# Expert weight loads of an up-projection spread out: at most two a step from step 25 to 30 in place of five at once

## The chip, the cores and the metric

One Trainium2 chip; the kernel runs on one of its cores. The metric is device time in microseconds (us). A core has five engines that run their own instruction streams and meet on semaphores: PE (TensorE, matmuls and transposes into PSUM), DVE (VectorE), ACT (ScalarE), POOL (GpSimd) and SP (SyncE), which here issues every DMA. "PEld" is the load of the stationary operand of a matmul.

## The reference, cut to what matters

Causal attention with a decay, a SiLU feed-forward layer, and a soft mixture of eight experts with four slots each, in fp32. `x` is 2304 tokens by 512.

```python
# attention (4 x 8 heads, 576 tokens, head 64) -> x (2304, 512)
h = x @ w_in                      # (2304, 2048)
g = h * (1.0 / (1.0 + np.exp(-h)))
x = g @ w_out                     # (2304, 512)

logits = x @ phi                  # 32 slots
d = softmax(logits, over tokens); c = softmax(logits, over slots)
slot_input = d.T @ x
for e in range(8):
    h = np.maximum(slot_input[e] @ w1[e], 0.0)     # w1[e]: 512 x 1024
    slot_out[e] = h @ w2[e]                        # w2[e]: 1024 x 512
return c @ slot_out
```

## The kernel before, in words

Attention comes first. The feed-forward layer is then run as 36 steps: nine chunks of 256 tokens times four groups of 512 hidden columns; a step is a pair (c, fg) and has a number k. Chunks 0 to 3 are interleaved in steps 0 to 15, and from step 16 on chunk 4 + (k - 16) // 4 is worked on, so that steps 24 to 27 are chunk 6, 28 to 31 chunk 7 and 32 to 35 chunk 8. The second matrix product is not carried out per token: `w_out` and `phi` are multiplied beforehand (tiles WP), and each step's `g` is used twice, for the logits (`lp`) and for the slot sums (`pp`).

A step on PE is: 24 matmuls `h` (two halves of 12, L593 to L595: three partial products of split operands), then `stacked(k)`: matmuls `lp` (L664) of the pieces that were made ready by the step before, perhaps `pp` (L780) for a whole chunk, and then `square(k)`: transposes `gtp` and small softmax pieces. ACT and DVE turn `h` into `gt` (L607, L614).

`lp` needs `g` transposed. There are two ways to it. `g_tr` transposes on PE (`gtp`, L637) and ACT copies the result into a tile `gr` (L638). The far way goes without PE: DVE transposes blocks of 32 by 32 into `gb` (`blocks`, L646), a DMA writes `gb` to a buffer `far` in HBM (L649), and four DMAs of 128 KB each bring it back as `gr` with the blocks in place (`placed`, L655). In steps 17 to 27 one or two pieces a step go the far way. `turn_far(k)`, at the end of `square(k)`, transposes them and issues the writes; `place(k + 1)`, in `stacked(k + 1)`, issues the reads; and `lp` of `stacked(k + 2)` uses them. Up to step 24 `gb` has a page of its own; from step 25 on it comes from a ring of two buffers (pool `w0`, tag `t`), which it shares with the `gr` of `g_tr`.

The pages: an allocator by hand, a list FREE of 4 KB-a-partition pages, first in, first out; `page()` takes one, `release()` gives it back when the last use has been recorded. `gt`, far `gr`, `xh`/`xl` (the split input) and the `unit` tiles all come from it.

A unit is 512 KB of weights for the tail: first eight that hold `w_out` (WO, written to HBM earlier), then 32 of `w1` and 32 of `w2`. `load_unit` (L442 for WO, L448 for `w1`, L450 for `w2`) issues one DMA on SP. How many may have been issued is set by the table ROOM, pairs of a step and a count, which is looked up at the end of each step:

```python
mo["umax"] = max([0] + [n for at, n in ROOM if k + 1 >= at])
pump()        # while len(WR) + len(units) < umax and FREE: load_unit()
```

All DMAs are on SP's queue in the order in which the program records them: reads, writes and units behind each other. Eight counters (DMAHW0 to DMAHW7) are given to them in turn, and an issue waits until the DMA that had the same counter eight issues before has landed. After step 35 the tail computes the experts (`h` L851 from `w1`, `so` L913 from `w2`) and combines.

Of the kernel before, what the change touches and what calls it, by code (L numbers as in the profile page):

```python
# [27 lines left out]
RATE = 1.5  # L28
CAPS = ((0, 12), (5, 6))
LAG = 1  # L30
ROOM = ((18, 5), (20, 6), (21, 7), (22, 10), (24, 11), (25, 12), (26, 17), (28, 19), (30, 23), (32, 29), (33, 32), (34, 35), (35, 42), (36, 45))
PARTS = ((0, 256, {}), (256, 128, {0: 1, 3: 2, 5: 2, 7: 2}), (384, 128, {1: 3, 3: 2, 5: 2, 7: 1}))
RING_A, RING_B, RING_T = "014", "235", "b"

# [2 lines left out]
def tile_attention_moe_softmoe(ctx: ExitStack, tc: tile.TileContext, qk, vr, f, wcat, phi, w1, w2, out):  # L37
# [394 lines left out]
    def pump():  # L432
        while mo["next"] < mo["last"] and mo["raws"] < mo["cap"] and len(FREE) > mo["spare"]:
            conv_dma()
        while len(WR) + len(units) < mo["umax"] and FREE:
            load_unit()
# [362 lines left out]
    def ct_page(c):  # L799
        t = page([96, 1024], "ct", F32R)[0]  # L800
        CTP.append(t)
        CT.update((c + k, t[:, 256 * k:256 * k + 256]) for k in range(4))
# [182 lines left out]
    with tc.manual_schedule():  # L985
# [156 lines left out]
        for k, (c, fg) in enumerate(steps):  # L1142
# [46 lines left out]
            if last:  # L1189
                ct_page(0)  # L1190
                ct_page(4)
            mo["umax"] = max([0] + [n for at, n in ROOM if k + 1 >= at])
            pump()
# [59 lines left out]
```

## Time and profile before

| | us |
|---|---|
| median of 3 runs | 536.84 |
| lowest and highest | 536.3, 539.62 |
| the profiled execution | 534.77 |
| its span, first to last instruction | 533.1 |
| PE busy in the span | 507.7 |
| mean granted TensorE clock, share of full | 0.994 |

The rows further down are from the profiled execution, 2.07 us below the median of the runs. Times in them count from the start of its span. Matmuls are pipelined and their ends are modelled, so each starts before the row before it has ended. A row with x8 is eight instructions merged, and its length includes the waits between them. In brackets stands how long the engine was idle before the row and what ended that.

### The profile page before, as it was taken

How to read it: one execution, taken by the hardware profiler on the slowest of the kernel's cores; microseconds unless marked ns; L12 is line 12 of the kernel's file. 1: busy time of each engine (PE TensorE's matmuls, PEld its weight loads, DVE VectorE, ACT ScalarE, POOL GpSimd, SP SyncE). 2: the span in 40 equal slices, each digit the busy share in tenths (PEclk: the TensorE clock that was granted, in tenths of full speed). 3: DMA queues.
4: the chain of work that ended last, by engine and by line, in shares of the span. 5: the costliest groups of instructions: out<-in, count | busy, mean ns of one | idle time of the engine just before them, and what ended most of it. 6: DMA issues, size and time to landing. Idle time of an engine off the chain costs nothing.

```text
span 533.1 us, 11562 instructions
## 1 busy us (share of the span) xinstructions
PE 507.7 (95%) x4285; PEld 373.7 (70%) x4285; DVE 336.6 (63%) x895; ACT 295.4 (55%) x586; POOL 208.4 (39%) x228
## 2 busy tenths in 40 slices
PE   8899999999999999899999999999998999999995
PEld 4687877787777787587777777757575667665563
DVE  6766777677789299999989534655654431434023
ACT  8798889889886675556645544323321333341012
POOL 9777788888788314447565300000000000001000
PEclk9999999999999999999999999999998999999998
DMA  5727656665553397213431119699697719767998
GB/s 145 222 79 204 194 169 172 180 190 156 147 173 96 110 347 287 80 41 101 137 119 79 41 49 317 188 297 260 229 333 204 256 65 337 254 255 302 408 405 310
DMA packets 44109, 105.83 MB, mean 199 GB/s; under 512 B 8180, under 2 KB 17172, under 8 KB 44052
## 3 DMA queue, kind: packets, MB, share of 16 engines
q1 hardware_dynamic: 44052, 105.08, 60.4%
q8 instruction: 34, 0.56, 0.4%
q14 instruction: 23, 0.19, 0.1%
HBM read 82.58 MB, written 17.52 MB: 188 GB/s over the span
## 4 chain that ended last, share of the span: by engine, by line
PE 61%; DMA 13%; DVE 11%; ACT 6%; POOL 3%; issue 3%; SPq 2%; DVEq 0%; POOLq 0%; ACTq 0%
PE h L593 8%; PE h L595 8%; PE h L594 8%; PE av L304 5%; DMA gr<-far 4%; PE st L247 3%; PE gtp L637 3%; PE mx L201 3%; PE lp L664 3%; PE rs L288 3%; PE st L249 3%; PE h L851 3%; PE pp L780 3%; PE so L913 3%; DMA QA<-mr 2%
## 5 line engine op out<-in xcount | busy, mean ns | idle before, releaser
L593 PE MATMUL h<-w,xh 128*128 128x512 f32 x288 | 118.8, 413 | 3.3 <-DVE gt L614 3.3
L595 PE MATMUL h<-w,xh 128*128 128x512 f32 x288 | 113.7, 395 | 0.0
L594 PE MATMUL h<-w,xl 128*128 128x512 f32 x288 | 113.5, 394 | 0.0
L614 DVE SCALAR_TENSOR_TENSOR gt<-gt,h 128x512 f32<-128x512 f32 (+1 forms) x73 | 48.4, 675 | 66.4 <-ACT gt L607 66.4
L607 ACT ACTIVATE gt<-h 128x512 f32<-128x512 f32 (+1 forms) x73 | 42.7, 589 | 80.6 <-PE h L595 68.8
L826 POOL MEMSET SM<- 128x512 f32 x2 | 1.1, 529 | 177.1 <-ACT gt L607 174.5
L253 ACT ACTIVATE E<-st 128x256 f32<-128x256 f32 (+4 forms) x160 | 63.2, 430 | 12.4 <-PE st L249 10.6
L593 PEld LDWEIGHTS h<-w,xh 128*128 128x128 f32 x288 | 54.2, 188 | 21.3 <-DVE gt L614 7.2
L207 DVE CUSTOM_DVE_ANT_0 junk<-mx,mask 128x64 bf16<-128x64 f32 (+3 forms) x128 | 49.9, 415 | 30.4 <-PE mx L201 27.5
L595 PEld LDWEIGHTS h<-w,xh 128*128 128x128 f32 x288 | 54.2, 188 | 12.7
L594 PEld LDWEIGHTS h<-w,xl 128*128 128x128 f32 x288 | 54.3, 189 | 10.8
L247 PE MATMUL st<-QA,KA 128*128 128x256 f32 (+2 forms) x192 | 55.7, 301 | 5.8 <-ACT E L253 2.8
L249 PE MATMUL st<-QB,KB 128*128 128x256 f32 (+2 forms) x192 | 51.6, 294 | 0.0
L201 PE MATMUL mx<-KA,QA 127*128 127x64 f32 (+2 forms) x192 | 49.7, 325 | 1.5 <-DVE Mt L207 0.7
L270 POOL TENSOR_SCALAR_AFFINE_SELECT E<-E 128x256 f32<-128x256 f32 (+1 forms) x96 | 40.9, 440 | 25.9 <-ACT E L253 24.5
L304 PE MATMUL av<-E,VF 128*64 128x320 f32 (+4 forms) x448 | 50.8, 364 | 0.0
L179 POOL TENSOR_TENSOR QB<-qk,QA 64x576 fp32r<-64x576 f32 x30 | 42.8, 1429 | 2.3
L177 POOL TENSOR_TENSOR KB<-qk,KB 64x576 fp32r<-64x576 f32 x30 | 42.2, 1425 | 1.7 <-ACT KB L171 0.6
L304 PEld LDWEIGHTS av<-E,VF 128*64 128x64 f32 x448 | 29.6, 137 | 17.8 <-POOL E L270 0.3
L247 PEld LDWEIGHTS st<-QA,KA 128*128 128x128 f32 x192 | 34.6, 180 | 10.5 <-ACT E L253 8.0
L524 POOL TENSOR_TENSOR raw<-raw 128x512 f32<-128x512 f32 x16 | 26.8, 1675 | 37.1 <-ACT raw L513 30.0
L201 PEld LDWEIGHTS mx<-KA,QA 127*128 127x128 f32 x192 | 32.8, 189 | 5.5 <-DVE Mt L207 2.0
(155 smaller groups left out, 854.5 us busy)
## 6 DMA issues: line engine op xcount, KB each, us to landing
unit<-in_w_dram SPq DMA_DIRECT2D x64, 512.0 KB
raw<-in_w_dram SPq DMA_DIRECT2D x32, 512.0 KB
far<-gb SPq DMA_DIRECT2D x16, 512.0 KB
gr<-far SPq DMA_DIRECT2D x64, 128.0 KB
qk<-in_qk_dram SPq DMA_DIRECT2D x14, 576.0 KB
VF<-in_v_dram SPq DMA_DIRECT2D x16, 320.0 KB
RB<-R SPq DMA_DIRECT2D x32, 144.0 KB
WO<-wt SPq DMA_DIRECT2D x8, 512.0 KB
```

What stands on the lines that cost most here:

```text
L179: eng.tensor_tensor(QB.of(p)[64:128, h], src[0:64], QA[p % 3][0:64, h, 64:640], ALU.subtract)
L201: nc.tensor.matmul(t[:, 0:w], lhsT=qa[0:127, h, 128 * blk:128 * blk + 128], rhs=ka[0:127, h, k0:k0 + w], start=True, stop=True)
L207: nc.vector.tensor_tensor_reduce(out=junk[:, 0:w], in0=t[:, 0:w], in1=mask[:, 448 - w:448], scale=1.0, scalar=Mx[p][:, h] if j == 5 else - ...
L247: nc.tensor.matmul(t[0:m, o:o + n], lhsT=ka[:, h, k0:k0 + m], rhs=qa[:, h, 64 + q0:64 + q1], start=True, stop=False)
L249: nc.tensor.matmul(t[0:m, o:o + n], lhsT=kb_[:, h, k0:k0 + m], rhs=qb[:, h, q0:q1], start=False, stop=True)
L253: nc.scalar.activation(e[0:m], t[0:m, 0:o], AF.Exp, scale=0.125)
L304: nc.tensor.matmul(AVP[p][x][64 * h:64 * h + 64, o0:o0 + n], lhsT=VF[p % 2][:, kb, h], rhs=E[2 * p + h][kb][:, c:c + n], start=kb == 0, st ...
L593: nc.tensor.matmul(o, lhsT=xh[:, d, tok], rhs=w[:, 0], start=(d == 0), stop=False)
L594: nc.tensor.matmul(o, lhsT=xl[:, d, tok], rhs=w[:, 0], start=False, stop=False)
L595: nc.tensor.matmul(o, lhsT=xh[:, d, tok], rhs=w[:, 1], start=False, stop=(d == 3))
L607: nc.scalar.activation(GT[c, fg][:, t, n * j:n * j + n], G[c, fg, t][:, n * j:n * j + n], AF.Tanh, scale=0.5)
L614: nc.vector.scalar_tensor_tensor(g, g, 1.0, h[:, n * j:n * j + n], op0=ALU.add, op1=ALU.mult)
```

## The change

The table ROOM is written anew between steps 26 and 31; nothing else differs. At the end of step 25 the count is 14 in place of 17, then 16 (17), 18 (19), 19 (19), 21 (23) and 23 (23) at the ends of steps 26 to 30. From step 31 on both tables are equal.

```diff
-ROOM = ((18, 5), (20, 6), (21, 7), (22, 10), (24, 11), (25, 12), (26, 17), (28, 19), (30, 23), (32, 29), (33, 32), (34, 35), (35, 42), (36, 45))
+ROOM = ((18, 5), (20, 6), (21, 7), (22, 10), (24, 11), (25, 12), (26, 14), (27, 16), (28, 18), (29, 19), (30, 21), (31, 23), (32, 29), (33, 32), (34, 35), (35, 42), (36, 45))
```

What SP's queue holds from the end of step 25 to step 28, before. `far<-gb` are the writes of the far way, `gr<-far` the reads (four a piece), `unit` the weight loads. The first row is the write of step 25, the five loads end that step, the four reads and two writes belong to step 26, the next three rows to step 27, and the last to step 28:

```order
L649 DMA far<-gb 128x1024
L448 DMA unit<-in_w_dram 128x1024 x5
L655 DMA gr<-far 32x4x256 x4
L649 DMA far<-gb 128x1024 x2
L655 DMA gr<-far 32x4x256 x8
L649 DMA far<-gb 128x1024
L448 DMA unit<-in_w_dram 128x1024 x2
L655 DMA gr<-far 32x4x256 x4
```

The same place on SP's queue in the changed program, from the write of step 25 on:

```order
L649 DMA far<-gb 128x1024
L448 DMA unit<-in_w_dram 128x1024 x2
L655 DMA gr<-far 32x4x256 x4
L649 DMA far<-gb 128x1024 x2
L448 DMA unit<-in_w_dram 128x1024 x2
L655 DMA gr<-far 32x4x256 x8
L649 DMA far<-gb 128x1024
L448 DMA unit<-in_w_dram 128x1024 x2
L655 DMA gr<-far 32x4x256 x4
```

Three loads have left the place ahead of the four reads of step 26, and two stand now between the two writes of step 26 and the eight reads of step 27, where there was none.

DVE executes the same instructions in the same order. What they wait for differs at the two transpositions of step 26 (a piece of the difference, the program before with -, the changed one with +; in brackets the counters waited for: DMAHW are landings, PE, DVE and Activation count instructions of these engines):

```order
 L797 TENSOR_TENSOR arena<-arena 128x64 [waits DVE_49]
 L646 STREAM_TRANSPOSE gb<-gt 128x1024 [waits DMAHW0_49]
-L646 STREAM_TRANSPOSE gb<-gt 128x1024 [waits DMAHW2_49,DVE_49]
-L614 SCALAR_TENSOR_TENSOR gt<-gt,h 128x512 [waits DMAHW5_49,DMAHW4_49,DMAHW6_49,DMAHW3_49,DMAHW7_49,DMAHW1_49,Activation_49]
+L646 STREAM_TRANSPOSE gb<-gt 128x1024 [waits PE_49]
+L614 SCALAR_TENSOR_TENSOR gt<-gt,h 128x512 [waits DMAHW2_49,DMAHW3_49,DMAHW1_49,Activation_49]
 L614 SCALAR_TENSOR_TENSOR gt<-gt,h 128x512 [waits Activation_49]
 L787 SCALAR_TENSOR_TENSOR arena<-arena,pp 128x512 [waits PE_49]
```

The second transposition of step 26 was put into the buffer of the first and waited until that one's write had landed. Now it is put into the buffer of step 26's `g_tr`, and waits until `lp` of step 27 has read that on PE.

## Rows read from the trace of the kernel before

**Rows 1.** The page's busy times and slices: engine, us, share, instructions; clock and DMA.

```profile
PE 507.7 (95%) x4285; PEld 373.7 (70%) x4285; DVE 336.6 (63%) x895; ACT 295.4 (55%) x586; POOL 208.4 (39%) x228
PEclk9999999999999999999999999999998999999998
```

**Rows 2.** PE from 356 to 421 us: start, length, line, instruction, [idle before].

```profile
356.89 0.40 PE L595 MATMUL h<-w,xh 128*128 128x512 f32 x1
358.28 1.07 PE L664 MATMUL lp<-gr,arena 128*32 128x256 f32 x16 [0.99 <-DMA gr<-far]
...
383.51 0.39 PE L595 MATMUL h<-w,xh 128*128 128x512 f32 x1
383.83 1.07 PE L664 MATMUL lp<-gr,arena 128*32 128x256 f32 x16
384.71 1.90 PE L780 MATMUL pp<-gt,arena 128*32 128x512 f32 x16
386.54 0.50 PE L593 MATMUL h<-w,xh 128*128 128x512 f32 x1
...
392.71 1.07 PE L664 MATMUL lp<-gr,arena 128*32 128x256 f32 x16
...
400.45 0.39 PE L595 MATMUL h<-w,xh 128*128 128x512 f32 x1
403.04 1.39 PE L664 MATMUL lp<-gr,arena 128*32 128x256 f32 x16 [2.20 <-DMA gr<-far]
404.13 3.39 PE L780 MATMUL pp<-gt,arena 128*32 128x512 f32 x16
407.45 0.50 PE L593 MATMUL h<-w,xh 128*128 128x512 f32 x1
...
413.63 1.07 PE L664 MATMUL lp<-gr,arena 128*32 128x256 f32 x16
...
420.69 0.64 PE L664 MATMUL lp<-gr,arena 128*32 128x256 f32 x8
```

**Rows 3.** The chain of work that ended last, 393 to 404 us: start, length, what.

```profile
395.30 7.64 DMA gr<-far
```

**Rows 4.** SP's queue of issues from 346 to 421 us.

```profile
346.23 1.47 SPq L649 DMA_DIRECT2D far<-gb  x2
347.74 0.46 SPq L442 DMA_DIRECT2D unit<-WO  x1
...
381.35 1.46 SPq L649 DMA_DIRECT2D far<-gb  x2
382.86 0.45 SPq L448 DMA_DIRECT2D unit<-in_w_dram  x1
...
389.39 2.72 SPq L448 DMA_DIRECT2D unit<-in_w_dram  x5
393.98 1.76 SPq L655 DMA_DIRECT2D gr<-far  x4
398.25 7.57 SPq L649 DMA_DIRECT2D far<-gb  x2
...
414.65 1.75 SPq L655 DMA_DIRECT2D gr<-far  x4
```

**Rows 5.** Stretches: length; busy of PE, PEld, DVE, ACT, POOL; clock, DMA share, GB/s.

```profile
356.00:358.00 2.00, 1.29 (x6) 0.72 (x4) 0.04 (x1) 0.60 (x1) 0.00 (x0) 1.00 1.09 344
358.00:360.00 2.00, 1.72 (x23) 1.22 (x24) 1.66 (x2) 0.40 (x2) 0.00 (x0) 1.00 1.01 414
...
396.00:398.00 2.00, 2.00 (x10) 1.60 (x9) 1.72 (x5) 0.14 (x1) 0.00 (x0) 1.00 1.03 412
...
404.00:406.00 2.00, 2.00 (x17) 0.71 (x12) 1.79 (x3) 0.18 (x1) 0.00 (x0) 0.50 0.03 8
...
430.00:440.00 10.00, 10.00 (x68) 6.47 (x68) 3.56 (x11) 3.13 (x6) 0.00 (x0) 1.00 0.14 43
```

**Rows 6.** DVE at the second transposition of step 26.

```profile
404.21 1.25 DVE L646 STREAM_TRANSPOSE gb<-gt 128x1024 f32<-128x1024 f32 x1 [5.99 <-DMA far<-gb]
```

## The prediction

> **What bounds the kernel now.** I read the page first. PE is busy for 507.7 of 533.1 us, and its granted clock shows one dip, in slice 31 of 40 [rows 1]. So the end is set by PE, and the places to look for are those where PE stands idle or is slowed. Then PE in order of time around the change. In steps 20 to 29 it waits once for more than a microsecond: `lp` of step 27 at 403.04 stood idle 2.20 us for its reads `gr<-far` [rows 2]. Compare the two stretches that run from the last `h` of a step over `lp` and `pp` to the first `h` of the next: 383.51 to 386.54 is 3.03 us in step 25, 400.45 to 407.45 is 7.00 us in step 27. The stage lost 3.97 us: 2.20 us of waiting, and in `lp` and `pp`, which took 1.39 and 3.39 us in place of 1.07 and 1.90, 1.81 us more [rows 2]. The stretch 404 to 406 has a granted clock of 0.50, the lower of the two levels, 1.2 GHz, after the engine had waited [rows 5]. An idle of 0.99 us before `lp` at 358.28 left the clock at 1.00 [rows 2, 5].
>
> The cause is on SP's queue. Five loads were issued from 389.39 on, the four reads of step 26 behind them at 393.98; the last of these reads took 7.64 us in the chain, from 395.30 to just before `lp` [rows 3, 4]. While loads alone flow, DMA moves 412 GB/s [rows 5], so a load of 524,288 bytes takes 1.27 us and five 6.4 us.
>
> **The change, part by part.** *Three loads leave the place ahead of the reads of step 26.* Two remain. The same arrangement (one write, two loads, four reads) stands in step 28 before: reads at 414.65, `lp` at 420.69 with no idle, so they landed in at most 6.04 us [rows 2, 4]. The reads of step 26 are issued once the write of step 25 has landed, which the change doesn't touch, at 393.98; they land by 400.02. `lp` of step 27 is due 0.32 us after the last `h` started (383.51 to 383.83 in step 25), at 400.77. The wait goes, with it the clock's dip: 3.97 us are saved up to there.
>
> *What is late next: `lp` of step 28.* It needs the eight reads of step 27, which need the two writes of step 26. Undisturbed, the first `h` of step 28 starts at 407.45 - 3.97 = 403.48, and `lp` is 6.18 us behind it (407.45 to 413.63; 6.17 in step 26, 386.54 to 392.71), so it is due at 409.66 [rows 2]. When are the reads there? The first transposition of step 26 doesn't move. The second one waited 5.99 us for the first one's write before, to 404.21 [rows 6]. Now it waits for the end of `lp` of step 27, as the order of DVE shows: 400.77 and 1.07 give 401.84. It takes 1.25 us, and the issue of the writes ended 0.36 us behind it before (405.46 to 405.82): 403.5 [rows 4, 6]. The two loads of step 26 are issued next, and the eight reads behind them.
>
> The time from the end of the issue of two writes to the landing of the eight reads comes from three places. With no load between, in step 27: 405.82 to `lp` at 413.63 without idle, at most 7.81 us. With one load, in step 25: 382.81 to 392.71 without idle, at most 9.90. With one load in step 21: 347.70 to 358.28, where `lp` waited, 10.58 [rows 2, 4]. With two loads, which no row shows, I bound it by 7.81 + 2 x 1.27 = 10.35 from below and by 10.58 + 1.27 = 11.85 from above (the second load at the rate of loads behind each other), and take 9.90 + 1.27 = 11.17, since step 25 is nearest in time and has loads of the same source. The reads land at 403.5 + 11.17 = 414.7 (413.9 to 415.4), and `lp` of step 28 waits 5.0 us (4.2 to 5.7).
>
> Whether reads stand behind loads is a question of the queue, and these rows answer it: with one load between, 2.1 to 2.8 us more passed than with none. The Trainium skill, in "DMA: Bandwidth & Descriptors", section "Queues, rings and completion order", says that each DMA engine takes descriptors in the order of its ring, and that all of SP's go into one row of rings. It speaks against the two loads at this place, and the trace agrees; a queue that let the reads pass would give the time of the first rival below.
>
> *The clock after this wait.* A wait of 2.20 us cost 1.81 us in slow matmuls behind it. One of 5.0 us isn't in the trace. Nothing if the clock stays up, as after 0.99 us; twice 1.81 if the low stretch grows in step with the wait. I take 1.81, because the work behind `lp` of step 28 is `h` matmuls, which fill PE as `pp` does, and the way back up begins with work, not with the wait.
>
> *Edits that cost nothing.* The loads held back (at most three at a time) are the 14th to 23rd; all 23 are out by the end of step 30 in both programs, and the tail uses them only after step 35. Between 430 and 440 us DMA is busy for 0.14 of its time, so two loads that come a step later have room [rows 5]; if that cover went, they would cost their 1.27 us each. The pages go to other tiles in the same first-in-first-out order, each released as before by `lp`, `pp` or `h` of a step already past, and from step 31 on the queue reads the same. Behind the second transposition DVE has the two `gt` of step 27, which the first `h` of step 28 waits for; before, they started at 405.46, now at 403.1, which ends the first by 403.8, some 0.3 us after that `h` is due, an estimate that I leave inside the bounds. `lp` of step 29 has four reads behind the write of step 27 and two loads; they are pushed back by about as much as `lp` of step 28 itself.
>
> **The sum.** Saved 3.97, new wait 5.0, slow clock behind it 1.8: 2.85 us more. With the bounds it is 0.3 (4.2 and no dip) to 5.3 (5.7 and 3.6). The profiled execution, 534.77, would become 537.6; it stands 2.07 below the median of the runs. Against that median, 536.84, I forecast 539.7 us (537.1 to 542.1), 0.5% slower. A difference under 1% (5.4 us) is about what a measurement of this kernel can't tell from no change.
>
> **The rivals.** *The reads aren't held up by the loads* (faster). If the reads of step 27 land in 7.81 us as with no load between, they are there at 411.3, `lp` of step 28 waits 1.65 us, which is nearer to the 0.99 that left the clock up, and the sum is -3.97 + 1.65 = -2.3: 534.5 us. For it speaks that the bounds for one load are upper bounds in two of three places; against it the 0.99 us in step 21, with a load that was a copy of WO. It decides from the point where the new wait and the slow matmuls behind it cost less than 3.97 us together.
>
> *The whole wait goes* (faster): the reads are there by 409.66, in 6.2 us from the writes, under anything the rows show. It needs the second transposition to run right behind the first, and the order says that it waits for `lp`. -3.97: 532.9 us.
>
> *A second wait behind it* (slower): the write of step 27 is issued only when the first of the eight reads has landed and is followed by two loads; if the four reads of step 28 are then late for `lp` of step 29 as well, I add a wait of the size seen, 2.2 us, and half of the 1.81 us that went with it: 2.85 + 2.2 + 0.9 = 5.95, 542.8 us. Against it: `lp` of step 29 moves back by the same 2.85 us.
>
> *The change doesn't do what it says*: excluded as to the order, which shows the loads moved.
>
> **How the numbers follow.** Forecast 0.68; reads not held up 0.16; whole wait gone 0.08; second wait 0.08. For the range I go down to the first rival (534.4) and up to 541.8, which leaves out the second rival, the third and the top of the forecast's own range, together some 0.2. Faster by over 1% would be under 531.5, which no case gives: 0.02. Slower by over 1% is over 542.2: the third rival and a little of the forecast, 0.11. Within 1%: 0.87.
>
> **What would show it.** In the changed profile: no idle before `lp` of step 27, at about 400.8; the second transposition of step 26 starting at about 401.9, its wait ended by `lp`; `lp` of step 28 idle for 4 to 6 us on `gr<-far`, at about 414.7; a granted clock of 0.5 behind that, no longer behind 403. I am wrong if reads land before 412, if the clock stays up there, or if anything from step 31 on differs by more than a shift.

## The result, and the profile after

The changed kernel takes 541.24 us (median of 20 runs, 536.49 to 544.71), the kernel before in the same comparison 537.58. The ratio is 1.0066, with a 95% interval from 1.0046 to 1.0086: slower by 3.5 us (2.5 to 4.6). The ratio leaves out the slowest of the 20 runs, 544.71 us, in which the chip was in a slower state. The profiled execution took 542.81 us with a span of 541.1.

PE of the changed kernel around the change: start, length, line, instruction, and in brackets how long it was idle before, and what ended that.

```profile
396.56 1.07 PE L664 MATMUL lp<-gr,arena 128*32 128x256 f32 x16
...
404.61 1.07 PE L664 MATMUL lp<-gr,arena 128*32 128x256 f32 x16
405.50 1.90 PE L780 MATMUL pp<-gt,arena 128*32 128x512 f32 x16
407.62 0.50 PE L593 MATMUL h<-w,xh 128*128 128x512 f32 x1 [0.23 <-DVE gt L614]
...
417.77 0.68 PE L664 MATMUL lp<-gr,arena 128*32 128x256 f32 x8 [3.86 <-DMA gr<-far]
419.78 1.08 PE L664 MATMUL lp<-gr,arena 128*32 128x256 f32 x8 [1.33 <-DMA gr<-far]
...
428.74 0.64 PE L664 MATMUL lp<-gr,arena 128*32 128x256 f32 x8
```

These answer to [rows 2]. `lp` of step 26 stands at 396.56 and stood at 392.71: this execution was 3.85 us later before the place of the change, where the programs are the same (over the ten profiled executions of this document that row starts between 392.71 and 396.86), so absolute times are read with that shift, and the change is read from stretches. From `lp` of step 26 to `lp` of step 27 is 8.05 us, 10.33 before: the wait of 2.20 us is gone, and `lp` and `pp` have their short lengths again. From `lp` of step 27 to that of step 28 the wait stands in its place: 3.86 us and, between the two pieces of `lp`, 1.33. From `lp` of step 26 to `lp` of step 29, the stage from here on, it is 428.74 - 396.56 = 32.18 us; before 27.98. That is 4.20 us more. From there to the end of the span it is 112.36 us, before 112.41: nothing moved behind the stage.

SP's queue, DVE, and the chain of work that ended last, in the changed kernel, one fence each:

```profile
397.23 1.75 SPq L655 DMA_DIRECT2D gr<-far  x4
402.08 5.28 SPq L649 DMA_DIRECT2D far<-gb  x2
407.48 1.19 SPq L448 DMA_DIRECT2D unit<-in_w_dram  x2
409.09 6.52 SPq L655 DMA_DIRECT2D gr<-far  x8
```

```profile
405.75 1.25 DVE L646 STREAM_TRANSPOSE gb<-gt 128x1024 f32<-128x1024 f32 x1 [3.70 <-PE lp L664]
```

```profile
407.94 7.35 DMA unit<-in_w_dram
415.31 4.23 DMA gr<-far
```

The second transposition of step 26, which waited for a write in [rows 6], waits for `lp`. Its write's issue ends at 402.08 + 5.28 = 407.36, the loads follow at once, and the chain runs from the second load to the last read, which lands at 419.54.

Stretches of the changed kernel with the granted clock (third figure from the end), DMA share and GB/s:

```profile
414.00:416.00 2.00, 0.00 (x0) 0.00 (x0) 0.69 (x1) 0.54 (x1) 0.00 (x0) 1.00 1.13 227
416.00:418.00 2.00, 0.23 (x5) 0.19 (x8) 0.00 (x0) 0.00 (x0) 0.00 (x0) 1.00 1.12 254
418.00:420.00 2.00, 0.67 (x12) 0.23 (x8) 0.00 (x0) 0.00 (x0) 0.00 (x0) 0.56 1.01 401
420.00:422.00 2.00, 2.00 (x12) 1.00 (x5) 0.67 (x4) 0.00 (x0) 0.00 (x0) 0.50 0.88 339
422.00:424.00 2.00, 2.00 (x6) 1.52 (x6) 0.83 (x5) 0.26 (x1) 0.00 (x0) 0.50 1.09 221
424.00:426.00 2.00, 2.00 (x8) 1.63 (x7) 0.00 (x0) 0.00 (x0) 0.00 (x0) 0.73 0.94 259
```

The clock falls to the lower level behind the wait of 3.86 us; four stretches in a row are below 1.00. From 414 to 418, in which the second load lands (415.31) and the last reads are under way, the DMA engines are wholly busy and move 227 to 254 GB/s, against 412 of loads alone [rows 5]. So low a rate needs no mixture of loads and reads: in the run below with all loads late, where no load is under way, these reads move 242 GB/s with the engines as busy:

```profile
408.00:410.00 2.00, 2.00 (x10) 1.65 (x9) 0.64 (x2) 0.60 (x1) 0.00 (x0) 1.00 1.01 242
```

### The profile page after: what moved, and what is told of

It is laid out like the page before. It is cut to its first block, busy times and chain, and to the rows that moved or that the text cites. A ratio compares the mean times of both kernels' runs of the same rounds, so it can differ in the third digit from the quotient of the medians.

```text
span 541.1 us, 11555 instructions
## 1 busy us (share of the span) xinstructions
PE 512.9 (95%) x4285; PEld 377.4 (70%) x4285; DVE 335.1 (62%) x895; ACT 296.6 (55%) x586; POOL 207.0 (38%) x228
## 4 chain that ended last, share of the span: by engine, by line
PE 67%; DVE 10%; ACT 7%; DMA 7%; POOL 3%; issue 3%; SPq 2%; DVEq 0%; POOLq 0%; ACTq 0%
PE h L593 9%; PE h L595 9%; PE h L594 9%; PE av L304 5%; PE mx L201 4%; PE st L247 4%; PE lp L664 4%; PE gtp L637 3%; PE st L249 3%; PE rs L288 3%; PE pp L780 3%; PE so L913 3%; PE h L851 3%; DMA gr<-far 3%; DVE wt L496 2%
## 5 line engine op out<-in xcount | busy, mean ns | idle before, releaser
L593 PE MATMUL h<-w,xh 128*128 128x512 f32 x288 | 120.0, 417 | 3.6 <-DVE gt L614 3.5
L595 PE MATMUL h<-w,xh 128*128 128x512 f32 x288 | 114.9, 399 | 0.0
L594 PE MATMUL h<-w,xl 128*128 128x512 f32 x288 | 114.7, 398 | 0.0
L253 ACT ACTIVATE E<-st 128x256 f32<-128x256 f32 (+4 forms) x160 | 63.6, 431 | 13.4 <-PE st L249 10.2
L593 PEld LDWEIGHTS h<-w,xh 128*128 128x128 f32 x288 | 55.1, 191 | 21.4 <-DVE gt L614 6.8
L595 PEld LDWEIGHTS h<-w,xh 128*128 128x128 f32 x288 | 54.9, 191 | 13.0
L201 PE MATMUL mx<-KA,QA 127*128 127x64 f32 (+2 forms) x192 | 50.8, 330 | 2.4 <-DVE mr L222 1.0
L524 POOL TENSOR_TENSOR raw<-raw 128x512 f32<-128x512 f32 x16 | 25.5, 1591 | 39.4 <-ACT raw L513 32.3
```

Source lines behind the costliest of these rows:

```text
L201: nc.tensor.matmul(t[:, 0:w], lhsT=qa[0:127, h, 128 * blk:128 * blk + 128], rhs=ka[0:127, h, k0:k0 + w], start=True, stop=True)
L253: nc.scalar.activation(e[0:m], t[0:m, 0:o], AF.Exp, scale=0.125)
L593: nc.tensor.matmul(o, lhsT=xh[:, d, tok], rhs=w[:, 0], start=(d == 0), stop=False)
L594: nc.tensor.matmul(o, lhsT=xl[:, d, tok], rhs=w[:, 0], start=False, stop=False)
L595: nc.tensor.matmul(o, lhsT=xh[:, d, tok], rhs=w[:, 1], start=False, stop=(d == 3))
```

## The experiments

The theory (A): the two loads at the end of step 26 and the late second transposition together make the new wait; each alone makes a smaller one. The rivals: the loads alone (B), the transposition alone (C). Ratios are against the kernel before, with 95% intervals.

**No loads at the end of step 26.**

```diff
-(26, 14), (27, 16), (28, 18), (29, 19), (30, 21), (31, 23)
+(26, 14), (28, 16), (29, 18), (30, 21), (31, 23)
```

> The two loads at the end of step 26 are moved to later steps (two each at the ends of steps 25, 27 and 28, three at 29, two at 30); the second transposition of step 26 still waits for lp of step 27. Theory A (loads and the late second write make the new wait together): the eight reads land some 7.8 us behind the second write's issue, lp of step 28 waits 1 to 2 us in place of 5.2, the clock stays up, lp of step 26 to lp of step 29 takes 25.5 to 26 us (before 28.0, changed kernel 32.2), ratio to the kernel before 0.995 to 0.997. Theory B (the loads alone): no wait at all, 24 us, 0.993. Theory C (the late second transposition alone): the wait stays at 5 us, 32 us, 1.006.

Ratio 0.9971 (0.9942 to 1.0). Its PE rows of `lp`, and the two writes on SP's queue:

```profile
393.76 1.07 PE L664 MATMUL lp<-gr,arena 128*32 128x256 f32 x16
...
412.75 0.64 PE L664 MATMUL lp<-gr,arena 128*32 128x256 f32 x8 [1.07 <-DMA gr<-far]
420.65 0.64 PE L664 MATMUL lp<-gr,arena 128*32 128x256 f32 x8 [1.20 <-DMA gr<-far]
```

```profile
399.29 5.28 SPq L649 DMA_DIRECT2D far<-gb  x2
```

`lp` of step 28 waits 1.07 us; the reads are there 412.75 - 404.57 = 8.2 us after the second write's issue. C falls (a wait of 5 us), and B does (no wait). A second wait of 1.20 us, at `lp` of step 29, wasn't expected: there the two loads of step 27 stand ahead of the four reads (more on this wait two runs below). The stage is 26.89 us, above the expected 25.5 to 26 by that wait.

**An own page for the second transposition of step 26, loads as changed.**

```diff
-                        blocks(*f, k < STEPS[1])
+                        blocks(*f, k < STEPS[1] or k == 26 and turns[2] < 1)
```

> Only the buffer of the second transposition of step 26 is changed: it gets a page of its own and no longer waits for lp of step 27; loads and queue stay as in the changed kernel. Theory A: the second write is issued some 3.7 us earlier, the reads behind two loads are still about 2 us late, lp of step 28 waits 1.5 to 3 us, lp 26 to lp 29 takes 26 to 28 us, ratio 0.996 to 1.000. Theory B (the loads alone): wait of 5 us as before, 32 us, 1.006. Theory C (the transposition alone): no wait, 24 us, 0.993.

Ratio 0.9972 (0.9945 to 0.9999).

```profile
395.26 1.07 PE L664 MATMUL lp<-gr,arena 128*32 128x256 f32 x16
...
414.49 0.64 PE L664 MATMUL lp<-gr,arena 128*32 128x256 f32 x8 [1.59 <-DMA gr<-far]
...
422.65 0.64 PE L664 MATMUL lp<-gr,arena 128*32 128x256 f32 x8
```

```profile
400.80 1.47 SPq L649 DMA_DIRECT2D far<-gb  x2
```

The second write's issue ends at 402.27, and the second piece of `lp` starts 12.2 us behind that; in the changed kernel it is 419.78 - 407.36 = 12.4. So what the page bought is the earlier start. The two times are nearly alike, but not made up alike. Here the second load waits 1.7 us for `lp` of step 27 (for its page, it seems), and SP then waits 0.8 us for a load to land while it issues the reads (2.9 in the changed kernel, shown further down):

```profile
SPq L448 <- PE lp L664: 1.7, 1, 1.7
SPq L655 <- DMA unit<-in_w_dram: 0.8, 1, 0.8
```

The wait falls from 5.19 to 1.59 us, at the low end of what A gave; the stage is 27.39 us. B and C fall again.

**Both edits**, the two diffs above.

> Both edits together: no loads at the end of step 26 and an own page for the second transposition. Theories A, B and C all expect no wait above 0.5 us at lp of steps 27 and 28, lp 26 to lp 29 in 24.0 us, ratio 0.9926. If the stage is 24 us and the ratio is not under 0.996, the time is lost again further on (the later loads).

Ratio 0.9955 (0.9928 to 0.9982). This missed what all theories expected:

```profile
396.86 1.07 PE L664 MATMUL lp<-gr,arena 128*32 128x256 f32 x16
...
413.85 1.07 PE L664 MATMUL lp<-gr,arena 128*32 128x256 f32 x16
422.89 0.64 PE L664 MATMUL lp<-gr,arena 128*32 128x256 f32 x8 [1.94 <-DMA gr<-far]
```

No wait at steps 27 and 28, but 1.94 us at step 29: the stage is 26.03 us, not 24.0. The two loads of step 27 stand ahead of the reads that this `lp` waits for, but they alone don't explain it. The kernel before has the same two loads there, and its `lp` of step 29 doesn't wait, though it comes 420.69 - 410.73 = 9.96 us behind the issue of step 27's write; without the wait it would come 10.5 us behind it here, and 10.0 us in the run with no loads at step 26. What differs is behind the reads: in both these runs seven loads follow, the first of them at once; in the kernel before the next load is issued 4.3 us behind the reads' issue. The rows are SP's queue in this run, and the loads of the kernel before:

```profile
413.88 1.75 SPq L655 DMA_DIRECT2D gr<-far  x4
415.73 10.64 SPq L448 DMA_DIRECT2D unit<-in_w_dram  x7
```

```profile
420.68 4.70 SPq L448 DMA_DIRECT2D unit<-in_w_dram  x4
```

Loads behind the reads alone make no wait either, as the next two runs show (eleven loads behind them). Which of the two this wait needs, or whether it needs both, no run parts.

**All eleven loads behind the last reads**, with the transposition as changed.

```diff
-(26, 14), (27, 16), (28, 18), (29, 19), (30, 21), (31, 23)
+(30, 23)
```

> All eleven loads of steps 25 to 30 are issued at the end of step 29, behind the last reads; the second transposition still waits for lp of step 27. Theory A: as without the two loads of step 26: a wait of 1 to 2 us at lp of step 28, 25.5 to 26 us from lp 26 to lp 29, ratio 0.995 to 0.997. Theory B: no wait, 0.993. Theory C: a wait of 5 us, 1.006. Against all three: if the loads are needed early, the tail waits for weights and the ratio is over 1.

Ratio 0.995 (0.9929 to 0.9972), stage 25.44 us, one wait of 0.89 us at `lp` of step 28, a little under the expected 1 to 2.

```profile
394.92 1.07 PE L664 MATMUL lp<-gr,arena 128*32 128x256 f32 x16
...
405.99 0.50 PE L593 MATMUL h<-w,xh 128*128 128x512 f32 x1 [0.22 <-DVE gt L614]
...
413.73 0.64 PE L664 MATMUL lp<-gr,arena 128*32 128x256 f32 x8 [0.89 <-DMA gr<-far]
...
420.36 0.64 PE L664 MATMUL lp<-gr,arena 128*32 128x256 f32 x8
```

No wait for weights appears in the tail: from `lp` of step 29 to the end of the span (533.2) it is 112.84 us, before 112.41.

**The loads behind the last reads and the own page**, the last diff and the one of the page.

> All eleven loads behind the last reads (end of step 29) and an own page for the second transposition of step 26, so that neither holds up a read. By the theory that both together made the wait: no idle before lp of steps 27, 28 and 29, lp 26 to lp 29 in 24.0 us (before 28.0, changed kernel 32.2), ratio to the kernel before 0.992 to 0.994. By the rival that late loads are paid later (tail waits for weights): stage 24 us, but ratio 0.997 or more.

Ratio 0.9931 (0.9903 to 0.9958), median 533.41 us: as expected, and faster than both kernels. `lp` of steps 26 to 29, none idle:

```profile
395.77 1.07 PE L664 MATMUL lp<-gr,arena 128*32 128x256 f32 x16
...
403.83 1.07 PE L664 MATMUL lp<-gr,arena 128*32 128x256 f32 x16
...
412.77 1.07 PE L664 MATMUL lp<-gr,arena 128*32 128x256 f32 x16
...
419.80 0.64 PE L664 MATMUL lp<-gr,arena 128*32 128x256 f32 x8
```

The stage is 24.03 us, with PE busy all through it at a granted clock of 1.00: 3.95 us less than before and 8.15 us less than in the changed kernel.

**One load and three loads at the end of step 26.** The tables are `(26, 14), (27, 15), (28, 17), ...` and `(26, 14), (27, 17), (28, 18), ...`.

> One load in place of two at the end of step 26 (the other goes to a later step). If every load between the writes and the reads costs the reads 2.1 us, as the runs with none (8.1 us from the second write to the last read) and two (12.3) say: 10.2 us, lp of step 28 waits 3.1 us. At the rate of loads behind each other, 1.27 us: 9.4 us and 2.3 us of waiting. If the place matters and not the number: 5.2 us.

> Three loads in place of two at the end of step 26 (one fewer at the end of step 27). At 2.1 us a load: 14.4 us from the second write to the last read, lp of step 28 waits 7.3 us, slower than the changed kernel by 2 us or a little more for the clock. At 1.27 us: 13.6 us and 6.5 us. If the place matters and not the number: 5.2 us as with two.

Ratios 1.0018 (0.9997 to 1.0039) and 1.0101 (1.0061 to 1.0141). `lp` of step 28 with one load, and the two writes:

```profile
414.08 0.64 PE L664 MATMUL lp<-gr,arena 128*32 128x256 f32 x8 [1.45 <-DMA gr<-far]
416.31 0.64 PE L664 MATMUL lp<-gr,arena 128*32 128x256 f32 x8 [1.58 <-DMA gr<-far]
```

```profile
400.82 5.27 SPq L649 DMA_DIRECT2D far<-gb  x2
```

The same with three:

```profile
417.31 1.08 PE L664 MATMUL lp<-gr,arena 128*32 128x256 f32 x8 [4.95 <-DMA gr<-far]
...
419.32 1.08 PE L664 MATMUL lp<-gr,arena 128*32 128x256 f32 x8 [0.92 <-DMA gr<-far]
```

```profile
400.55 5.27 SPq L649 DMA_DIRECT2D far<-gb  x2
```

From the end of the second write's issue to the second piece of `lp`: 8.2 us with no load, 10.2 with one, 12.4 with two, 13.5 with three. The first two cost 2.0 and 2.2 us each, the third 1.1, less than the 2.1 expected; the waits are 3.03 us (expected 3.1) and 5.87 (expected 7.3). The number matters, not only the place. Each figure is from one profiled execution of its run.

**The two loads at their place with an eighth of their bytes.**

```diff
-            nc.sync.dma_start(out=t, in_=w1[e, q * 128:(q + 1) * 128])
+            n = 128 if j in (6, 7) else 1024
+            nc.sync.dma_start(out=t[:, 0:n], in_=w1[e, q * 128:(q + 1) * 128, 0:n])
+            if n < 1024:
+                REST.append((t[:, n:1024], w1[e, q * 128:(q + 1) * 128, n:1024]))
...
+            if k == 29:
+                for o, i in REST:
+                    nc.sync.dma_start(out=o, in_=i)
```

> The two loads of step 26 stay at their place, but bring only 128 of 1024 columns (64 KB each); the rest of both is loaded at the end of step 29, so that the result is the same. If the bytes ahead of the reads make the delay: an eighth of 4.2 us, some 0.5 us, is left, lp of step 28 waits 1.6 us, close to the run without loads at step 26 (1.07). If it is the issue on SP and the counters that the reads then share with loads: 4 to 5.2 us as in the changed kernel.

Ratio 0.9988 (0.9967 to 1.0009).

```profile
415.45 0.64 PE L667 MATMUL lp<-gr,arena 128*32 128x256 f32 x8 [1.54 <-DMA gr<-far]
```

The wait is 1.54 us, where the bytes gave 1.6 and the issues and counters 4 to 5.2. So it is the bytes ahead of the reads that delay them, not two more issues. How the bytes do it stays open in one point: with whole loads, the last reads also take counters that the loads hold until they land (the chain above passes from the load to the last read at 415.31). SP's waits for a load to land, while it issues the eight reads, are (total us, times, longest) with one, two and three whole loads:

```profile
SPq L655 <- DMA unit<-in_w_dram: 1.0, 1, 1.0
SPq L655 <- DMA unit<-in_w_dram: 2.9, 2, 2.0
SPq L655 <- DMA unit<-in_w_dram: 3.5, 3, 2.0
```

With no load and with the two short ones there is no such wait. So 1.0 of 2.0, 2.9 of 4.2 and 3.5 of 5.3 us of the delay are seen as late issue of the last reads. Whether reads issued at once would have landed sooner, behind the same bytes, no run shows: with short loads the bytes and the wait for counters go together.

## Why the prediction was right

The sign, the mechanism and its place came out; the sizes behind the new wait were too small, and the wait itself fits better than its parts. Step by step:

- *The wait at step 27 goes.* Forecast 400.77 for its `lp`; measured 404.61 less the shift of 3.85, that is 400.76. Worth 3.97 us by the forecast; the run without any wait gives 27.98 - 24.03 = 3.95.
- *The second write of step 26.* Forecast to be issued by 403.5; 407.36 less 3.85 is 403.51. DVE waits for `lp`, as its row says.
- *The reads of step 27.* Forecast 11.17 us behind that; the last landed 12.2 us behind, over the upper bound of 11.85. The mis-sized term is the load: the second was counted at the 1.27 us of loads behind each other, and at this place it costs 2.2 (the first 2.0). The forecast's lower bound stood on 7.81 us, itself only an upper bound; with no load it measured 8.2.
- *The wait at step 28.* Forecast 5.0 us; 3.86 + 1.33 = 5.19, in two pieces. That it fits so well is partly luck: the last read landed 1.0 us later than forecast, but `lp` was due 0.4 us later as well (417.77 - 3.86 - 3.85 = 410.06, forecast 409.66), and half of it was carried out in between.
- *The clock.* Forecast 1.81 us. The stage is 8.15 us over the run without waits; less 5.19 of waiting for reads and 0.23 for DVE (forecast: some 0.3, left out of the sum), 2.73 are left. Not all of it is the clock: with all loads late, the same reckoning leaves 25.44 - 24.03 - 0.89 - 0.22 = 0.30 us, at a granted clock of 1.00 throughout the stage. So some 2.4 us are slow matmuls, an estimate inside the bound of 3.6. Of the 1.35 us that the sum was short of, these are some 0.6; the 0.3 beside them, DVE and the longer wait make up the rest.
- *The sum.* 2.85 forecast, 4.20 in the stage of the profiled execution, 3.5 (2.5 to 4.6) in the timed runs. The forecast time, 539.7 us, stands on a median of 536.84; in the comparison the kernel before had 537.58, and the changed kernel 541.24. That a difference under 1% can't be told from none was too cautious: with 20 runs of each kernel, 0.66% is clear of noise.
- *The loads held back cost nothing* (they are the 15th to 23rd, not the 14th to 23rd), and nothing moves from step 29 to the end: 112.36 us against 112.41.

Of the rivals, reads that pass the loads are excluded by the runs with none to three loads. That the whole wait goes is excluded by DVE's row: the second transposition waited 3.70 us for `lp`. The second wait, at `lp` of step 29, didn't come in the changed kernel, where that `lp` had moved back, as the reason given has it. It came, at 1.20 and 1.94 us, in two runs in which step 28 waited less or not at all, but these also had loads right behind the reads, so that reason isn't shown by itself.

## What to carry to other kernels

Spreading a burst evenly over steps helps only if the new places have room: what counts is not how many loads a step has but what stands behind each on the queue, and how long that is from its use. Look at what follows the transfer at once, too: the waits at step 29 came only in runs with loads on both sides of the reads. Put bulk loads behind the last transfer that a near step needs, not between a write and its reads. When such a move changes which buffer a ring gives out, look at what the new wait is for.

## What the hardware did that was not expected

- A load of 512 KB ahead of reads of 128 KB pieces delayed them by 2.0 and 2.2 us (the first two) and 1.1 us (the third), while at the 412 GB/s of loads alone it takes 1.27 us. The reads, with no load beside them, moved 242 GB/s with the DMA engines wholly busy.
- The length of a wait alone didn't tell whether the clock falls. After 1.59 us (own page, loads as changed) it was at the lower level, in the first row below; after 1.94 us (both edits) it stayed up, in the second. The rows are stretches of the two runs.

```profile
416.00:418.00 2.00, 2.00 (x7) 1.51 (x6) 0.96 (x5) 0.26 (x1) 0.00 (x0) 0.50 1.01 286
```

```profile
422.00:424.00 2.00, 1.11 (x16) 0.65 (x20) 0.31 (x1) 0.35 (x1) 0.00 (x0) 1.00 0.95 363
424.00:426.00 2.00, 2.00 (x20) 0.98 (x13) 0.64 (x1) 0.16 (x2) 0.00 (x0) 1.00 0.83 279
```
